# Routing steps spread over the attention passes of a fused attention and expert kernel

## The chip, the cores and the metric

The kernel runs on one core of one Trainium2 chip. The metric is the time of one execution on the device in microseconds (us), the median of several runs. A core has five engines that run at the same time and wait for each other by semaphores: TensorE (PE in the profile, its loads of weights PEld), VectorE (DVE), ScalarE (ACT), GpSimd (POOL) and SyncE (SP), which here only issues transfers. 16 DMA engines move data between the chip's memory (DRAM) and the core's SBUF; transfers are issued by SP, ACT and POOL. Products land in PSUM, from which VectorE and ScalarE read.

## The reference

Two stages. First attention with a mask by blocks, for 8 batches and 8 heads, 576 rows of 64; then a layer of 8 experts over all 4608 tokens (512 wide, the hidden width 1024), in which each token goes to one expert:

```python
scores = scale * np.matmul(q, k.transpose(0, 1, 3, 2))
scores = np.where(block_i >= block_j, scores, -1e9)        # blocks of 64 rows
attn = softmax(scores)                                     # minus the row's maximum, exp, over the sum
x = (attn @ v), heads side by side                         # 8 x 576 x 512
fresh_e = argmax(x[b, s] @ w_gate)
e = fresh_e if s == 0 or sigmoid(x[b, s] @ w_local) < 0.5 else prev_e
p = softmax(x[b, s] @ w_gate)
out[b, s] = p[e] * (relu(x[b, s] @ w1[e]) @ w2[e])
```

The expert of a token can be that of the token before, so the choice is a running recurrence along a batch's tokens.

## The kernel before, in words

**Attention in passes.** A pass works on one batch and a pair of heads: 32 passes (NPR), in a loop over `it` from -2 to 31. In each turn of it three passes are under way: `a = it + 2` is transposed (turns, tails), `c = it + 1` has its row maxima taken (top, mid_maxima, high_maxima), and `e = it` goes through scores, exp (segment, expo) and the products with v (av, L659 and L667); the pass before, `x = it - 1`, is brought back to rows (norm, cast_x, rows_x) and written to a table of rows in DRAM (x_rows). Row maxima are reduced by VectorE out of PSUM (L577 to L581), exchanged between halves of the partitions by GpSimd or VectorE (exchange, L590 to L592), and turned into a diagonal (shift, L599) that TensorE subtracts from the scores. GpSimd also casts the transposed queries to bf16 (halves_in, L992).

**Gate and routing, beside the passes.** Every fourth pass TensorE adds up the gate's sums for the batch (gate_sums, L732). The tokens fall into four groups of 9 x 128 (GC = 9 columns of 128 tokens). For a group the routing is a chain of small operations: gate and fresh (the fresh expert), fresh_b, rows_ps and scan_rows (the recurrence as a scan over rows), carry, chosen (one-hot rows of the chosen expert), ranks, ranks_all and ranks_b (the token's place among its expert's tokens), shares (its weight p), and, for the first two groups together, whole, tile_experts, taken, low1 and high (which slot of which tile a token gets; TensorE inverts the table by products of one-hot rows, inverse, L380).

**The order is written by hand.** The kernel is in manual order: each engine runs its instructions as the program emits them. The dictionary `plan` holds for a pass `it` and a named place a list of pieces, entered with `at(it, place, piece)` and run by `run(it, place)`. In the order of a pass the places are: start, mid (behind the middle maxima, ahead of two segments), top, begin, turned (inside tails), turn, gap (ahead of the last query blocks' products and their norm_last, L541), late (behind norm_last; then come the other products, and in the next pass norm, L533), end, first (TensorE's part of the routing). The pieces of group g begin at pass `i0 = 8 * g + 9 + g // 2`.

**Weights.** The experts' weights come by GpSimd's queue in quarters (weights, load_weights, L63), spread over the passes, the last ones at passes 28 to 30. The last pass also starts the experts: three gathers of rows (gather, L763), DMA transposes (turn_rows, L784), and copies of the first two experts' w1 (first, L779).

**Experts in tiles.** A tile is 128 tokens of one expert. For tile t: gather, turn_rows, first (VectorE copies w1 of an expert whose offset is read at run time), up (32 products, L798), down (8 products with w2 at an offset read at run time, L813), scatter (L822). 36 tiles run in a loop; `steps`, `ahead` and `behind` hold the routing pieces of the later groups for each t; up to 7 more tiles run if they are used.

**Start.** `warm(n)` issues n products of ones into a scratch tile of PSUM (L837) ahead of the first transposes.

Of the kernel before, what the change touches and what calls it, by code (L numbers as in the profile page):

```python
# [16 lines left out]
def kernel(  # L17
# [28 lines left out]
    P = 128  # L46
# [127 lines left out]

    def fresh_b(g):
        best = sm9[:, 1, :]
        nc.vector.tensor_mul(tmp["eq"], tmp["eq"], desc_e[:, None, :].to_broadcast([P, GC, E]))
        nc.vector.reduce_max(best, tmp["eq"], axis=AX)
        nc.vector.tensor_scalar(best, best, -1.0, float(E), op0=ALU.mult, op1=ALU.add)
        nc.vector.tensor_mul(ak[:, 0, :], best, sm9[:, 2, :])  # L180
# [81 lines left out]
    def ranks_all(g):  # L262
        off = sm9[:, 4, 0:E]
        nc.vector.tensor_add(tmp["pf"], tmp["pf"], off[:, :, None].to_broadcast([P, E, GC]))
        nc.vector.tensor_add(tmp["pf"], tmp["pf"], tots[:, 0, :].rearrange("p (e c) -> p e c", c=GC))
        nc.vector.tensor_mul(tmp["pf"], tmp["pf"], ohg(g))

    def ranks_b(g):
        rk = sm9[:, 5, :]
        nc.vector.reduce_sum(rk, over_e(tmp["pf"]), axis=AX)  # L270
        nc.vector.tensor_copy(ints[:, 0, 0, :], rk)
        nc.vector.tensor_single_scalar(ints[:, 1, 0, :], ints[:, 0, 0, :], 7,
# [26 lines left out]

    def per_token(dst, w, n, tmp):  # L300

        nc.vector.tensor_mul(tmp, oh[:, :, 0:n], w[:, :, None].to_broadcast([P, E, n]))
        nc.vector.reduce_sum(dst, over_e(tmp), axis=AX)
# [123 lines left out]
    with tc.manual_schedule():  # L427
# [428 lines left out]
        warm(26)  # L856
# [21 lines left out]
        def low1(g, z):  # L878
            c0, n = GC * g + 5 * z, 5 - z
            low(ohl01[:, c0:c0 + n, :], c0, n)  # L880

        at(29, "first", lambda ps: inverse(ps, None, rhsa, na, NTA))
        for g in range(3):
            i0 = 8 * g + 9 + g // 2
            at(i0, "turn", lambda ps, g=g: gate(g))
            at(i0, "late" if g == 2 else "gap", lambda ps, g=g: fresh(g))
            at(i0 + 1, "gap", lambda ps, g=g: fresh_b(g))
            at(i0 + 1, "first", lambda ps: rows_ps(ps, buf))
            at(i0 + 2, "gap", lambda ps: scan_rows(buf))
# [11 lines left out]
            if g == 2:  # L901
                at(i0 + 5, "gap", lambda ps, g=g: ranks(g))
                at(i0 + 5, "gap", lambda ps, g=g: ranks_all(g))
                at(i0 + 5, "end", lambda ps, g=g: ranks_b(g))
# [5 lines left out]
            at(i0 + 7, "gap", lambda ps, g=g: ranks_b(g))  # L910
            at(i0 + 8 if g else i0 + 7, "late", lambda ps, g=g: shares_b(g))
# [16 lines left out]
        at(30, "turn", lambda ps: weights(2))  # L928
# [8 lines left out]
        for it in range(-2, NPR):  # L937
# [30 lines left out]
            def turns():  # L968

                pw[:] = g_tile(0), g_tile(1)  # L970
                if a == 0:
                    for w in (1, 0):
# [4 lines left out]
                        turned(0, w, pw[w])  # L977
                    return
# [260 lines left out]
        def highb():  # L1239
# [18 lines left out]
                     lambda: fresh_b(last)],  # L1258
# [6 lines left out]
                     lambda: ranks_in(cur[2], dve), lambda: ranks(last), lambda: ranks_all(last)],  # L1265
                 10: [lambda: ranks_b(last), plan2],
# [14 lines left out]
        for t in range(NTM):  # L1281
            for z in (3, 4, 5) if t == 0 else wait_for.get(t, (t + 5,)):
                if z < NTM + 2:
                    gather(z)
            if t + 1 < NTM:
# [8 lines left out]
            for f in ahead.get(t, []) + steps.get(t, []):  # L1294
# [65 lines left out]
```

## Time and profile before

| | |
|---|---|
| median of three runs | 458.43 us (458.36 to 460.65) |
| the profiled execution | 454.2 us, span 452.4 us |
| TensorE busy | 432.8 us (96%) |
| VectorE, ScalarE, GpSimd busy | 315.1, 273.6, 288.5 us |
| mean granted TensorE clock | 0.995 |
| DMA | 71.15 MB, mean 157 GB/s |

The passes run from about 11 us to 304 us of the span, the experts from 305 us to the end. A line of the timeline reads: start and duration in us, engine, line of the kernel, operation, output <- input with sizes, how many are merged, and in brackets how long the engine had been idle and what ended that. In the view by stretches each engine has its busy time and its count of instructions; then come the granted clock (1.00 is full), the share of the DMA engines and GB/s.

### The profile page before, as it was taken

To read this page: it belongs to the slowest core of one execution; us is meant where nothing else is said; L and a number is where in the kernel's file an instruction comes from. 1 tells how busy PE (TensorE), PEld (TensorE's weight loads), DVE (VectorE), ACT (ScalarE), POOL (GpSimd) and SP (SyncE) were. 2 spreads that over 40 slices of the span, in tenths; PEclk is the share of its full clock that TensorE was granted. 3 is DMA by queue.
4 is the path that set the end of the run, shared out by engine and by line. 5 is a ranking of instruction groups with operands and counts; after the bars stand their busy time and mean duration, and the time that the engine had idled before them with its cause. 6 is when DMAs were issued, how large, how long until landed. Compare 5 with 4: busy or idle time off the path is not lost.

```text
span 452.4 us, 19648 instructions
## 1 busy us (share of the span) xinstructions
PE 432.8 (96%) x7738; PEld 338.2 (75%) x7738; DVE 315.1 (70%) x856; ACT 273.6 (60%) x573; POOL 288.5 (64%) x674
## 2 busy tenths in 40 slices
PE   7899999999999999999999999987999999999994
PEld 5688787787788877787878777776676777777772
DVE  4777667768778888887788897954876884333422
ACT  3857766766667657665766666554454555555552
POOL 4556566667566747675556665672777758878853
PEclk8999999999999999999999999999999999999999
DMA  8999699999999975999779898887655665546532
GB/s 152 190 164 188 143 173 164 195 186 171 185 181 175 186 162 117 203 161 183 158 143 184 149 179 152 146 139 104 146 137 153 137 147 149 151 130 167 141 116 80
DMA packets 169885, 71.15 MB, mean 157 GB/s; under 512 B 151424, under 2 KB 158080, under 8 KB 169792
## 3 DMA queue, kind: packets, MB, share of 16 engines
q1 hardware_dynamic: 154640, 38.05, 44.5%
q0 software_dynamic: 13952, 31.52, 34.4%
q8 instruction: 64, 1.05, 1.0%
q10 hardware_dynamic: 1200, 0.30, 0.3%
q14 instruction: 29, 0.24, 0.2%
HBM read 67.18 MB, written 14.97 MB: 182 GB/s over the span
## 4 chain that ended last, share of the span: by engine, by line
PE 41%; DVE 26%; POOL 12%; issue 11%; DMA 5%; ACT 2%; POOLq 1%; DVEq 0%; ACTq 0%
PE g L667 10%; DVE mx L577 9%; PE ps_s L625 8%; POOL out_dram L822 6%; PE ps_s L634 4%; PE ps_h L798 4%; DMA out_dram<-o_sb,tok2s 3%; PE g L659 3%; PE ps_m L558 3%; PE ps_o L813 3%; PE g L951 2%; PE g L732 2%; DVE diag L599 2%; POOL diag L599 1%; DMA x_rows<-w_bf 1%
## 5 line engine op out<-in xcount | busy, mean ns | idle before, releaser
L641 ACT ACTIVATE prob<-ps_s 128x640 f32<-128x640 f32 (+2 forms) x128 | 103.6, 839 | 41.3 <-PE ps_s L634 40.4
L577 DVE TENSOR_REDUCE mx<-ps_m 128x2 f32<-128x640 f32 (+2 forms) x96 | 100.2, 1044 | 26.9 <-PE ps_m L558 19.9
L625 PE MATMUL ps_s<-plb 64*128 64x320 f32 (+4 forms) x768 | 107.3, 400 | 0.7 <-DVE mx L579 0.7
L625 PEld LDWEIGHTS ps_s<-plb 64*128 64x128 f32 x768 | 68.0, 189 | 20.8 <-issue 9.8
L667 PE MATMUL g<-vt,prob 128*64 128x65 f32 x2560 | 80.3, 222 | 0.0
L667 PEld LDWEIGHTS g<-vt,prob 128*64 128x64 f32 x2560 | 77.5, 138 | 0.1
L813 PE MATMUL ps_o<-w_bf,hT 128*128 x304 | 71.5, 380 | 0.0
L802 ACT ACTIVATE hT<-ps_h 128x512 bf16<-128x512 f32 x76 | 45.4, 597 | 26.6 <-PE ps_h L798 26.2
L816 ACT ACTIVATE o_sb<-ps_o,share 128x512 f32<-128x512 f32 x37 | 25.4, 686 | 40.2 <-PE ps_o L813 35.7
L813 PEld LDWEIGHTS <-hT 128*128 128x128 bf16 x304 | 28.0, 98 | 27.8 <-issue 0.3
L590 POOL COPY mx<-mx 64x2 f32<-64x2 f32 x64 | 11.7, 183 | 52.3 <-DVE mx L581 49.7
L779 DVE COPY natb<-w_bf 128x4096 bf16 x20 | 24.7, 1235 | 27.5 <-PE ps_h L798 25.2
L779 DVE COPY plb<-w_bf 128x4096 bf16 x20 | 25.1, 1253 | 24.6 <-PE ps_h L798 24.1
L798 PEld LDWEIGHTS <-plb 128*128 128x128 bf16 x608 | 35.4, 98 | 6.8 <-issue 2.9
L798 PEld LDWEIGHTS <-natb 128*128 128x128 bf16 x608 | 35.4, 98 | 6.2 <-DVE rs L541 1.5
L558 PE MATMUL ps_m<-kh,qh 64*128 64x320 bf16 (+3 forms) x256 | 37.6, 324 | 2.5 <-DVE mx L581 1.4
L634 PE MATMUL ps_s<-diag,ones 64*128 64x448 bf16 (+1 forms) x372 | 36.8, 274 | 2.0 <-DVE diag L599 0.4
L822 POOL DMA_INDIRECT out_dram<-o_sb,tok2s x17 | 28.7, 1690 | 11.6 <-ACT o_sb L816 7.0
L63 POOL DMA_DIRECT2D w_bf<-in_moe_w_dram x56 | 33.4, 596 | 1.4 <-DMA x_rows<-xb 0.4
L987 ACT COPY plb<-g 128x512 f32<-128x512 f32 x62 | 33.2, 593 | 0.3 <-PE g L951 0.2
L651 POOL MEMSET prob<- 64x128 f32 x128 | 24.5, 206 | 11.1 <-ACT prob L641 5.0
L798 PE MATMUL ps_h<-scr,plb 128*128 128x128 bf16 x416 | 25.3, 219 | 2.6 <-DVE share L788 2.3
(285 smaller groups left out, 769.8 us busy)
## 6 DMA issues: line engine op xcount, KB each, us to landing
w_bf<-in_moe_w_dram POOLq DMA_DIRECT2D x48, 256.0 KB, 4.5
vt<-in_v_dram SPq DMA_DIRECT2D x64, 128.0 KB
natb<-in_k_dram SPq DMA_DIRECT2D x63, 128.0 KB
natb<-in_q_dram SPq DMA_DIRECT2D x63, 128.0 KB
w_bf<-in_moe_w_dram POOLq DMA_DIRECT2D x8, 512.0 KB, 5.5
x_rows<-w_bf SPq DMA_DIRECT2D x13, 256.0 KB
natb<-in_k_dram SPq DMA_DIRECT2D x32, 32.0 KB
vt<-in_v_dram SPq DMA_DIRECT2D x32, 32.0 KB
```

Source lines behind the costliest of these rows:

```text
L63: nc.gpsimd.dma_start(out=dst[:, e * WE:(e + 1) * WE].rearrange("p (k f) -> p k f", k=n)[:, r:r + m, :], in_=view[e][:, r:r + m, :])
L558: nc.tensor.matmul(ps[:, h, c:c + w], lhsT=qh[rows(h), 64 * b:64 * b + 128], rhs=kh[rows(h), 0:w], start=True, stop=m is None)
L577: nc.vector.reduce_max(mx[:, b:b + 2], ps[:, :, 0:w], axis=AX)
L625: nc.tensor.matmul(ps[:, h, c:c + n], lhsT=pls[i][rows(h), S + 128 * j:S + 128 * j + 128], rhs=pls[i][rows(h), a:a + n], start=part == 0, ...
L634: nc.tensor.matmul(ps[:, h, c:c + n], lhsT=ones[rows(h), :], rhs=diag[rows(h), a // 64:(a + n) // 64, :], start=False, stop=part == len(SE ...
L641: nc.scalar.activation(p[:, :, SEG0[s]:SEG0[s] + w], ps[:, :, 0:w], func=AF.Exp, scale=scale_attn)
L667: nc.tensor.matmul(g[rows(e), o + 65 * h:o + 65 * h + 65], lhsT=p[:, h, c:c + 64], rhs=t[:, j, h, :], start=(j == 0), stop=(j == m))
L779: nc.vector.tensor_copy(w, w1_bf[:, bass.ds(off, WE)])
L798: nc.tensor.matmul(ps_h[:, f, :], lhsT=w[:, f0 + ko * F:f0 + ko * F + 2 * P - 1:2], rhs=xb[:, ko * P:(ko + 1) * P], start=(ko == 0), stop= ...
L802: nc.scalar.activation(hT[:, half * 4:half * 4 + 4, :], ps_h, func=AF.Relu)
L813: nc.tensor.matmul(ps_o, lhsT=hT[:, fo, :], rhs=w2_bf[:, bass.ds(woff + fo * Dm, Dm)], start=(fo == 0), stop=(fo == FO - 1))
L822: wr = nc.gpsimd.indirect_dma_start(out=out_flat, out_offset=bass.IndirectOffsetOnAxis(ap=g[1][:, g[3]:g[3] + 1], axis=0), in_=o_sb, in_of ...
```

## The change

The pieces of the routing are cut finer and put at other places of the passes, some of them on another engine; a weight load moves, and the start gets more products of ones.

- fresh_b loses its product and its reduce to a new fresh_a. For groups 0 and 1 fresh_a runs in mid, for group 2 in the gap. fresh(2) moves from late to the gap of pass 26, scan_rows(2) from the gap to mid of pass 28.
- ranks_all loses its last product to ranks_own, ranks_b its first two operations to ranks_a. For groups 0 and 1 ranks_own runs in mid, ranks_a in the gap (pass 16 and 25), ranks_b in late of the same pass.
- shares_b of groups 0 and 1 runs on GpSimd.
- low1, the one-hot rows of a token's low part, was one VectorE operation for 5 or 4 columns; it becomes 5 or 4 GpSimd operations of 128 x 128. For group 1 it moves from passes 28 and 29 to late of 26 and 27.
- whole moves from late of 23 to the gap of 24, tile_experts from the gap to mid of 25; taken is cut into four pieces in mid and late of 26 and 27; taken_b moves from late of 27 to the gap of 28.
- The last weight load, weights(2) in the last pass, moves into the expert loop, behind the gather of tile 3 (the fourth).
- At t = 1 of the expert loop the steps run ahead of `sums`.
- At the start half of the first qh is copied by ScalarE instead of VectorE; warm(26) becomes warm(29), and warm(5) and warm(8) stand between and behind the first transposes.

```diff
+    def fresh_a(g):
+        nc.vector.tensor_mul(tmp["eq"], tmp["eq"], desc_e[:, None, :].to_broadcast([P, GC, E]))
+        nc.vector.reduce_max(sm9[:, 1, :], tmp["eq"], axis=AX)
...
+    def ranks_own(g):
         nc.vector.tensor_mul(tmp["pf"], tmp["pf"], ohg(g))
...
-    def shares_b(g):
+    def shares_b(g, eng=nc.vector):
         for j in range(3):
-            nc.vector.tensor_copy(sh[:, :, j], pgs)
+            eng.tensor_copy(sh[:, :, j], pgs)
             if j < 2:
-                nc.vector.tensor_sub(pgs, pgs, sh[:, :, j])
+                eng.tensor_tensor(pgs, pgs, sh[:, :, j], op=ALU.subtract)
...
-            for c in (0, 256):
-                nc.vector.tensor_copy(qh[:, c:c + 256], ps[:, c:c + 256])
+            nc.vector.tensor_copy(qh[:, 0:256], ps[:, 0:256])
+            nc.scalar.copy(qh[:, 256:512], ps[:, 256:512])
...
-        warm(26)
+        warm(29)
...
-            low(ohl01[:, c0:c0 + n, :], c0, n)
+            for c in range(c0, c0 + n):
+                nc.gpsimd.tensor_scalar(ohl01[:, c, :], iota_lo, hl[:, 1, c:c + 1], 0.0,
+                                        op0=ALU.is_equal, op1=ALU.add)
...
-            at(i0, "late" if g == 2 else "gap", lambda ps, g=g: fresh(g))
+            at(i0, "gap", lambda ps, g=g: fresh(g))
+            at(i0 + 1, "gap" if g == 2 else "mid", lambda ps, g=g: fresh_a(g))
...
-            at(i0 + 2, "gap", lambda ps: scan_rows(buf))
+            at(i0 + 2, "mid" if g == 2 else "gap", lambda ps: scan_rows(buf))
...
-            at(i0 + 7, "gap", lambda ps, g=g: ranks_b(g))
-            at(i0 + 8 if g else i0 + 7, "late", lambda ps, g=g: shares_b(g))
+            at(i0 + 7, "mid", lambda ps, g=g: ranks_own(g))
+            at(i0 + 8 if g else i0 + 7, "gap", lambda ps, g=g: ranks_a(g))
+            at(i0 + 8 if g else i0 + 7, "late", lambda ps, g=g: ranks_b(g))
+            at(i0 + 8 if g else i0 + 7, "late", lambda ps, g=g: shares_b(g, nc.gpsimd))
...
-        at(23, "late", lambda ps: whole(False))
+        at(24, "gap", lambda ps: whole(False))
         at(24, "late", lambda ps: whole_b(NTA))
-        at(25, "gap", lambda ps: tile_experts(tea, tend, NTA, tmpta))
-        at(26, "gap", lambda ps: taken(t1ka, hia, na, tmpa))
-        at(27, "late", lambda ps: taken_b(t1ka, hia, na))
-        at(28, "turn", lambda ps: low1(1, 0))
+        at(25, "mid", lambda ps: tile_experts(tea, tend, NTA, tmpta))
+        at(26, "mid", lambda ps: per_token_a(t1, na, tmpa))
+        at(26, "late", lambda ps: per_token_b(t1ka, tmpa))
+        at(26, "late", lambda ps: low1(1, 0))
+        at(27, "mid", lambda ps: per_token_a(dd, na, tmpa))
+        at(27, "late", lambda ps: per_token_b(hia, tmpa))
+        at(27, "late", lambda ps: low1(1, 1))
+        at(28, "gap", lambda ps: taken_b(t1ka, hia, na))
...
-        at(29, "gap", lambda ps: low1(1, 1))
...
-        at(30, "turn", lambda ps: weights(2))
...
                         turned(0, w, pw[w])
+                        warm(5 * w)
...
                 g1 = tails()
+                warm(8)
                 tails_in()
...
             for z in (3, 4, 5) if t == 0 else wait_for.get(t, (t + 5,)):
                 if z < NTM + 2:
                     gather(z)
+                if z == XGB:
+                    weights(2)
...
-            for f in ahead.get(t, []) + steps.get(t, []):
+            for f in steps.get(t, []) + ahead.get(t, []) if t == 1 else ahead.get(t, []) + steps.get(t, []):
                 f()
```

More of the change, by code (lines that the diff above doesn't have):

```diff
@@ L903 @@
                 at(i0 + 5, "gap", lambda ps, g=g: ranks_all(g))
+                at(i0 + 5, "gap", lambda ps, g=g: ranks_own(g))
+                at(i0 + 5, "end", lambda ps, g=g: ranks_a(g))
                 at(i0 + 5, "end", lambda ps, g=g: ranks_b(g))
@@ L1264 @@
                      lambda: new_g(1, lambda ps: ranks_ps(last, ps)),
-                     lambda: ranks_in(cur[2], dve), lambda: ranks(last), lambda: ranks_all(last)],
-                 10: [lambda: ranks_b(last), plan2],
+                     lambda: ranks_in(cur[2], dve), lambda: ranks(last), lambda: ranks_all(last),
+                     lambda: ranks_own(last)],
+                 10: [lambda: ranks_a(last), lambda: ranks_b(last), plan2],
                  11: [plan2_a, lambda: plan2_b(tmp2, hi2)],
```

15 lines of the change are left out of this document (9 added, 6 removed).

## The prediction

> **What bounds the kernel now.** I read the page first (engines, chain), then the timeline pass by pass, then the waits in the two places where the passes end and the experts begin.
>
> ```profile
> PE 432.8 (96%) x7738; PEld 338.2 (75%) x7738; DVE 315.1 (70%) x856; ACT 273.6 (60%) x573; POOL 288.5 (64%) x674
> PE 41%; DVE 26%; POOL 12%; issue 11%; DMA 5%; ACT 2%; POOLq 1%; DVEq 0%; ACTq 0%
> ```
>
> TensorE is busy for 96%, yet the chain that ended last runs over VectorE and GpSimd for 38% of the span: TensorE is the bound with little slack to the other two. So I look for passes that are longer than a clean one. A mark for each pass is the first product of the last query block (L659). Here is a clean pass, 73.43 to 82.02, with VectorE's three waits in it:
>
> ```profile
> 73.43 0.74 PE L659 MATMUL g<-vt,prob 128*64 128x65 f32 x18
> 75.28 0.18 DVE L541 RECIPROCAL rs<-g 128x3 f32<-128x3 f32 x1 [1.11 <-PE g L667]
> 76.61 0.20 DVE L533 RECIPROCAL rs<-g 128x6 f32<-128x6 f32 x1 [0.56 <-PE g L667]
> 79.13 1.23 DVE L577 TENSOR_REDUCE mx<-ps_m 128x2 f32<-128x1024 f32 x1 [0.54 <-PE ps_m L558]
> 82.02 0.80 PE L659 MATMUL g<-vt,prob 128*64 128x65 f32 x20
> ```
>
> 8.59 us. VectorE idles 1.11 us in the place that the plan calls "gap", 0.56 us in "late", 0.54 us in "mid". Routing work in gap and late is free up to 1.67 us together; beyond that it pushes L533 (3.18 us after the mark here). The mid wait is a product's latency and stays when VectorE is late, so work of 0.5 us there is free, while a late L533 lengthens the pass one for one. The marks where routing runs (the pass after each mark):
>
> ```profile
> 109.02 0.80 PE L659 MATMUL g<-vt,prob 128*64 128x65 f32 x20
> 118.38 0.80 PE L659 MATMUL g<-vt,prob 128*64 128x65 f32 x20
> 227.66 0.56 PE L659 MATMUL g<-vt,prob 128*64 128x65 f32 x11
> 237.25 0.80 PE L659 MATMUL g<-vt,prob 128*64 128x65 f32 x20
> 247.34 0.80 PE L659 MATMUL g<-vt,prob 128*64 128x65 f32 x20
> 256.77 0.80 PE L659 MATMUL g<-vt,prob 128*64 128x65 f32 x20
> 265.87 0.80 PE L659 MATMUL g<-vt,prob 128*64 128x65 f32 x20
> 274.81 0.81 PE L659 MATMUL g<-vt,prob 128*64 128x65 f32 x20
> 285.39 0.80 PE L659 MATMUL g<-vt,prob 128*64 128x65 f32 x20
> 294.63 0.80 PE L659 MATMUL g<-vt,prob 128*64 128x65 f32 x20
> 93.75 1.22 PE g L732 x30
> ```
>
> The last row is the gate sums, 1.22 us of TensorE in every fourth pass (it = 24 and 28 here). Above 8.59, or 9.81 with sums: it 10 +0.77, it 23 +1.00, 24 +0.28, 25 +0.84, 26 +0.51, 27 +0.35, 28 +0.77, 29 +0.65. The check of the reading is the pass from 247.34: the next fence has its L533 at 251.42, 4.08 after the mark, 0.90 later than in the clean pass, and the pass is 0.84 longer.
>
> **The change, part by part.**
>
> *Routing pieces off VectorE's gap and late.*
>
> ```profile
> 109.86 1.24 DVE L177 TENSOR_TENSOR scr<-scr,desc_e 128x72 f32<-128x72 f32 x1
> 231.26 0.23 DVE L266 TENSOR_TENSOR scr<-scr,oh 128x72 f32<-128x72 f32 x1
> 251.42 0.19 DVE L533 RECIPROCAL rs<-g 128x6 f32<-128x6 f32 x1
> 275.46 0.82 DVE L366 TENSOR_TENSOR ohl<-hl,iota_lo 128x640 bf16<-128x640 f32 x1
> 277.24 0.41 DVE L193 TENSOR_TENSOR_SCAN scr<-scr,zeros 9x128 f32<-9x128 f32 x1
> ```
>
> - it 10: fresh_a (the 1.24 us product and a reduce) leaves the gap for mid; the two small operations and this step's transposes on TensorE stay. Of +0.77 I take away 0.45.
> - it 15 and 23: the product of ranks_own leaves late (0.23 and its spacing, 0.26 each); from it 23 also whole's three smaller operations (under L266's 0.23 each; 0.46 together). 0.26 + 0.72.
> - it 24: ranks leaves the gap, whole's half microsecond comes in, whole_b stays in late under the sums: the 0.28 goes, less 0.03: 0.25.
> - it 25: the table's three operations go from the gap to mid, behind a stretch with sums, where there is room; ranks_a's two come into the gap; shares_b's five small dependent operations go to GpSimd, ranks_b's three come into late (two fewer, about 0.4). With the gap's relief L533 comes back nearly to 3.18: 0.80 of 0.84.
> - it 28 and 29: the one-hot rows (0.82 in it 28, the smaller one in it 29) leave VectorE. In it 28 taken_b's five small operations come into the gap, which they fit. 0.72 of 0.77; in it 29 0.31 of 0.65, since the inverse's products and the carry stay.
>
> - it 26 and 27: the four operations of taken go in pairs to mid and late (a reduce of 144 elements in late is covered by its 0.56); fresh and fresh_a stand in the gap, as much as it holds. it 27 keeps its +0.35, which its transposes on TensorE would set anyway. 0 beyond what follows.
>
> Sum: 0.45 + 0.26 + 0.72 + 0.25 + 0.80 + 0.72 + 0.31 = 3.5 us less. A piece costed at nothing in mid (ranks_own twice, per_token_a twice) is covered by the 0.54; without that cover each costs its length (0.23 for L266, the others wider).
>
> What mid costs: scan_rows in it 28 is two scans of 0.41 and a memset (about 0.9 us, over the 0.5 by 0.4), and an operation with two inputs there holds up GpSimd's exchange that starts at the same time (fence below). I take +0.6 for both, between 0 and 1.5 (every mid piece in full beyond the 0.54).
>
> *One-hot rows on GpSimd.* Eighteen operations of 128x128 (5 in it 17, 4 in 18, 5 in 26, 4 in 27) stand behind the pass's second weight load and ahead of the exchange of the next pass's middle maxima, whose chain (exchange, L599, the cast of qh) TensorE waits for without slack.
>
> ```profile
> 78.73 0.18 POOL L590 COPY mx<-mx 64x2 f32<-64x2 f32 x1 [1.40 <-DVE mx L581]
> 82.45 0.29 POOL L1036 CAST qh<-plb 128x128 bf16<-128x128 f32 x1
> 176.56 0.79 POOL L591 COPY mx<-mx 64x2 f32<-64x2 f32 x1
> 179.34 0.18 POOL L590 COPY mx<-mx 64x2 f32<-64x2 f32 x1 [0.20 <-DVE mx L581]
> ```
>
> No row shows such an operation on GpSimd. Lower end: 0.18 (L590's); nearest in shape: 0.29 (the 128-column cast); upper: 0.79 (L591, a copy that usually takes 0.18 and stood behind VectorE's 0.82 us one-hot). I take 0.27 start to start, just under the cast, since independent ones overlap: 1.35 us for five. In a clean pass GpSimd has 1.40 us free ahead of the exchange (78.73). In it 17 the gate stands there too, and 0.20 us are left (179.34); 0.61 come back, since L591 is no longer held, and about 0.36 go, since VectorE delivers earlier: room 0.45, so the five make the exchange 0.9 late. VectorE's own lateness in this pass goes (0.82 in late against 0.56 of idle time, about 0.3): net +0.6. In it 26, which has the gate as well, +0.51 becomes +0.9: +0.4. In it 18 and 27 there is no gate, and four fit into 1.40: 0. Together +1.0 (at 0.18 an operation about +0.1, at 0.5 +4.5).
> [...]
>
> *The last weight rows behind the fourth gather.*
>
> ```profile
> 299.00 0.79 POOL L63 DMA_DIRECT2D w_bf<-in_moe_w_dram  x1
> 302.04 1.86 POOL L763 DMA_INDIRECT xg<-x_rows,toka  x1 [0.16 <-issue]
> 305.08 1.11 PE L798 MATMUL ps_h<-scr,natb 128*128 128x128 bf16 x17 [1.42 <-DMA scr<-scr]
> 309.30 0.89 PE L798 MATMUL ps_h<-scr,plb 128*128 128x128 bf16 x13 [2.27 <-DVE share L788]
> 311.89 1.90 PE L813 MATMUL ps_o<-w_bf,hT 128*128 x8
> L813 PEldq EVENT_SEMAPHORE  x2: 51/51/51, 310.5 to 310.7; - x2
> DMA to landing us min/median/max: 4.1/4.5/5.5
> ```
>
> TensorE waits 1.42 us for the first transposed rows and 2.27 us before the second tile (VectorE's share is not read by it, so I take this to be the second transpose too). The 512 KB load of 299.0 is in the queues just then. Without it both tiles could follow at once: 3.7 us. But the first L813 reads a slice at an offset known only at run time, so it waits for every load of w2 (the two semaphore events stand ahead of the first L813 alone), and everything on TensorE stands behind it. The load now starts behind the gather of 302.04, at about 304.2, and lands 5.5 us later, 309.7, or up to 311.5 beside the other transfers; gathers 4 and 5 are pushed by about 0.8 and are wanted later. (304.2 is 302.04 + 1.86 and 0.3 for the issue.) So L813 moves from 311.89 to 309.8 at best. I take 310.5: -1.4, between -2.1 and +1.0.
>
> *Table work ahead of the sums (t = 1), and ones in the gaps of the start.*
>
> ```profile
> 316.30 0.52 DVE L744 TENSOR_TENSOR lgS<-g,lgS 128x128 f32<-128x128 f32 x2 [3.79 <-PE g L732]
> 320.25 1.23 DVE L779 COPY natb<-w_bf 128x4096 bf16 x1 [0.26 <-issue]
> 322.06 1.95 PE L798 MATMUL ps_h<-scr,natb 128*128 128x128 bf16 x32 [0.46 <-DVE tmp L302]
> 3.90:7.31 3.41, 2.07 (x21) 1.26 (x21) 0.76 (x2) 1.85 (x7) 0.10 (x1) 1.00 1.30 193
> 7.31:10.73 3.42, 3.42 (x30) 1.86 (x26) 2.50 (x5) 0.36 (x1) 2.30 (x9) 0.50 0.72 154
> 10.71 1.23 DVE L577 TENSOR_REDUCE mx<-ps_m 128x2 f32<-128x1024 f32 x1 [0.74 <-PE ps_m L558]
> ```
>
> whole_b and the shares go into VectorE's 3.79 us of idling; the copy of 320.25 starts over 2 us earlier and TensorE's 0.46 us goes: -0.4 (0 to -0.5).
> At the start the granted clock is 0.50 from 7.31 to 10.73 (the last columns are clock, DMA, GB/s), after 3.41 us in which TensorE was busy for 2.07. Sixteen more products of ones (3, 5 and 8; 0.056 each, as seventeen of that shape take 1.11 at 305.08) bring some 0.9 us into that stretch. With the clock full VectorE's 0.74 us wait goes; the eight ahead of the first scores cost up to 0.45. Half of qh runs on ScalarE beside VectorE's half; no row prices that, and I leave it inside the range. I take -0.5, between -1.2 and +0.4.
> [...]
>
> **Sum:** -3.5 + 0.6 + 1.0 - 1.4 - 0.4 - 0.5 = -4.2 us. The profiled execution took 454.2 us (span 452.4 and 1.8 around it), 4.2 less than the median of the runs, 458.43. The terms are differences inside one execution, and behind the passes TensorE runs without a gap, so I subtract them from the median: 454.2 us, -0.9%.
>
> **Rivals.**
> 1. The seam gives nothing, since L813 waits for the moved load (landing at 311.5 to 312) or the second transpose lands as late as before. For it: the two semaphore events; against: 5.5 us of landing. Seam 0 to +0.8: 455.6 to 456.4.
> 2. GpSimd becomes the bound (slower than before): each one-hot operation takes 0.79 as L591 did. The five run 3.5 us past their room of 0.45, the four 1.8 past 1.4: 10.6 us instead of my 2 x 0.9, so 458.4 - 4.2 + 8.8 = 463. It decides against the change from 0.54 us an operation: 2 x (5 x 0.54 - 0.45) + 2 x (4 x 0.54 - 1.4) - 0.83 = 5.2, all the rest of the sum. [...]
> 3. The pieces don't move out of the way: mid is no idle stretch, because the chain runs through it. Each mid piece then costs its length: fresh_a 0.5 twice, ranks_own 0.25 twice, per_token_a (two larger products) about 0.33 twice, scan_rows 0.9, together 3.1 instead of 0.6: 456.7. Against it: 0.54 us in a clean pass, after TensorE's product.
>
> **How the numbers follow.** Forecast 0.51 (own range 452.3 to 455.6), rival 1 0.21, rival 2 0.14, rival 3 0.14. This kernel's runs spread by 0.5% (458.36 to 460.65), 2.3 us; that is my bound for no change, 456.1 to 460.7. Faster: 0.51, most of rival 1 (0.12) and little of rival 3 (0.02), 0.65. Slower: rival 2 with over 0.67 us an operation and the tails, 0.12. Same: the rest, 0.23. The best ends of all terms (mid 0, one-hot rows +0.1, seam -2.1, sums -0.5, start -1.2) give -7.2, 451.2; I set that as low, and 459.0 high, which leaves out rival 2's upper part and the tails, under 2 in 10.
>
> **What would show it.** Right: the passes after marks 10, 15, 23, 25 and 28 within 0.35 of 8.59 (9.81); those of it 17 and 26 longest, with GpSimd's one-hot rows directly ahead of L590; both expert waits under 0.5 us and a new one ahead of the first L813; no stretch at 0.50 behind 7.3; no wait at the fifth tile. Wrong: one-hot rows above 0.5 us, VectorE's L577 without its wait behind a mid piece and the pass longer, or L813 not earlier against the gather.

## The result, and the profile after

| | before | after |
|---|---|---|
| median of the runs | 458.39 us | 465.01 us |
| ratio | | 1.0117, 95% 1.0074 to 1.0159 |
| the profiled execution | 454.2 us, span 452.4 | 462.77 us, span 461.1 |
| VectorE, GpSimd busy | 315.1, 288.5 us | 308.7, 295.2 us |

The change makes the kernel slower by 1.2%; a second measurement of the same pair (below) gave 1.0086, 1.0061 to 1.0111. One of the four runs after lay in a slower state of the chip and the ratio leaves it out: the other three have a median of 463.85 us. The forecast was 454.2 us, 0.9% faster. On the page of the changed kernel (busy time of each engine, then the chain that ended last):

```profile
PE 436.3 (95%) x7754; PEld 340.8 (74%) x7754; DVE 308.7 (67%) x841; ACT 271.4 (59%) x574; POOL 295.2 (64%) x702
PE 51%; DVE 15%; POOL 12%; issue 11%; DMA 6%; ACT 3%; POOLq 1%; DVEq 0%; ACTq 0%
```

VectorE did lose its place in the chain (26% before, 15% now) and 6.4 us of work; still the span grew. The timeline of the changed kernel says where. L670 is the line of the pass marks (L659 before):

```profile
109.56 0.63 PE L670 MATMUL g<-vt,prob 128*64 128x65 f32 x14
118.47 0.80 PE L670 MATMUL g<-vt,prob 128*64 128x65 f32 x20
174.07 0.80 PE L670 MATMUL g<-vt,prob 128*64 128x65 f32 x20
185.56 0.63 PE L670 MATMUL g<-vt,prob 128*64 128x65 f32 x14
194.94 0.80 PE L670 MATMUL g<-vt,prob 128*64 128x65 f32 x20
231.10 0.80 PE L670 MATMUL g<-vt,prob 128*64 128x65 f32 x20
239.95 0.28 PE L670 MATMUL g<-vt,prob 128*64 128x65 f32 x2
249.84 0.34 PE L670 MATMUL g<-vt,prob 128*64 128x65 f32 x4
258.52 0.80 PE L670 MATMUL g<-vt,prob 128*64 128x65 f32 x20
270.67 1.35 PE L670 MATMUL g<-vt,prob 128*64 128x65 f32 x20
280.18 0.80 PE L670 MATMUL g<-vt,prob 128*64 128x65 f32 x20
306.89 0.75 PE L670 MATMUL g<-vt,prob 128*64 128x65 f32 x20
```

Passes 10, 23 and 25 came down as forecast (8.91, 8.85 and 8.68 us against a clean 8.59). Pass 17 takes 11.49, 18 takes 9.38, 26 takes 12.15 and 27 takes 9.51: 8.17 us over four clean passes, 1.50 before. The last mark is 5.6 us later than before (306.89 against 301.28). Pass 17 in the timeline, with GpSimd's rows and the TensorE row that waits for them (L892 is the one-hot row, L601 the exchange, L625 VectorE's first operation behind the exchange, L1013 the cast of qh; rows may overlap where several are merged):

```profile
178.96 1.44 POOL L892 TENSOR_SCALAR ohl<-iota_lo,hl 128x128 bf16<-128x128 bf16 x2
179.68 2.78 POOL L892 TENSOR_SCALAR ohl<-iota_lo,hl 128x128 bf16<-128x128 bf16 x4
182.53 0.18 POOL L601 COPY mx<-mx 64x2 f32<-64x2 f32 x1
182.99 0.16 DVE L625 TENSOR_TENSOR mx<-mx 128x1 f32<-128x1 f32 x1 [1.44 <-POOL mx L602]
184.12 0.60 POOL L1013 CAST qh<-plb 128x512 bf16<-128x512 f32 x1
184.77 0.31 PE L569 MATMUL ps_m<-kh,qh 64*128 64x320 bf16 x2 [3.00 <-POOL qh L1013]
```

Five operations fill GpSimd from 178.96 to 182.47, 0.70 us each; the exchange follows at once, then shift and cast, and TensorE stands still for 3.00 us. The view of waits (us in total, times, longest) names the same chain, and one new wait for the weight load:

```profile
PE ps_m L569 <- POOL qh L1013: 6.6, 3, 3.0
PE ps_o L824 <- DMA w_bf<-in_moe_w_dram: 2.5, 1, 2.5
```

The start of the experts in the changed kernel (L63 the moved load, L809 first layer, L824 second layer):

```profile
309.12 0.78 POOL L63 DMA_DIRECT2D w_bf<-in_moe_w_dram  x1
309.55 0.62 PE L809 MATMUL ps_h<-scr,natb 128*128 128x128 bf16 x8
311.35 0.83 PE L809 MATMUL ps_h<-scr,plb 128*128 128x128 bf16 x12
314.16 1.04 PE L824 MATMUL ps_o<-w_bf,hT 128*128 x4
317.65 1.02 PE L824 MATMUL ps_o<-w_bf,hT 128*128 x4 [2.45 <-DMA w_bf<-in_moe_w_dram]
318.72 1.50 PE L809 MATMUL ps_h<-xb,natb 128*128 128x128 bf16 x24
323.01 1.17 PE L809 MATMUL ps_h<-scr,plb 128*128 128x128 bf16 x18
326.53 1.67 PE L809 MATMUL ps_h<-scr,natb 128*128 128x128 bf16 x27
```

Both first-layer waits are gone, the second layer's first four products run, and the fifth waits for the load, which lands 8.5 us after its issue. The third tile starts 11.83 us behind the last mark, 12.34 before; the fifth 3.52 us behind the fourth, 4.14 before. After that the profiled execution loses about 4 us for which the profile shows no cause (from the fourth tile's last product to the last product of all it takes 124.8 us); a second trace of the same kernel takes 120.9 there, as before the change, so the change does not bring them every time.

### The profile page after: what moved, and what is told of

Same layout as the page of the kernel before. It is cut to its first block, busy times and chain, and to the rows that moved or that the text cites. A ratio compares the mean times of both kernels' runs of the same rounds, so it can differ in the third digit from the quotient of the medians.

```text
span 461.1 us, 19695 instructions
## 1 busy us (share of the span) xinstructions
PE 436.3 (95%) x7754; PEld 340.8 (74%) x7754; DVE 308.7 (67%) x841; ACT 271.4 (59%) x574; POOL 295.2 (64%) x702
## 4 chain that ended last, share of the span: by engine, by line
PE 51%; DVE 15%; POOL 12%; issue 11%; DMA 6%; ACT 3%; POOLq 1%; DVEq 0%; ACTq 0%
PE g L678 12%; PE ps_s L636 8%; DVE mx L588 7%; PE ps_h L809 6%; PE ps_o L824 5%; PE ps_s L645 4%; PE g L670 4%; PE ps_m L569 3%; DMA out_dram<-o_sb,tok2s 3%; POOL out_dram L833 3%; PE g L971 2%; PE g L743 2%; POOL ohl L892 2%; POOL scr L774 2%; POOL xg L774 2%
## 5 line engine op out<-in xcount | busy, mean ns | idle before, releaser
L678 PE MATMUL g<-vt,prob 128*64 128x65 f32 x2560 | 81.4, 222 | 0.5 <-issue 0.4
L824 PE MATMUL ps_o<-w_bf,hT 128*128 x304 | 71.8, 379 | 2.8 <-DMA w_bf<-in_moe_w_dram 2.5
L813 ACT ACTIVATE hT<-ps_h 128x512 bf16<-128x512 f32 x76 | 43.9, 596 | 40.2 <-PE ps_h L809 23.2
L824 PEld LDWEIGHTS <-hT 128*128 128x128 bf16 x304 | 28.0, 98 | 31.4 <-issue 4.1
L809 PEld LDWEIGHTS <-natb 128*128 128x128 bf16 x608 | 35.5, 98 | 6.6 <-issue 2.5
L809 PEld LDWEIGHTS <-plb 128*128 128x128 bf16 x608 | 35.5, 98 | 5.1 <-issue 1.1
L601 POOL COPY mx<-mx 64x2 f32<-64x2 f32 x64 | 11.8, 185 | 42.4 <-DVE mx L592 36.8
L63 POOL DMA_DIRECT2D w_bf<-in_moe_w_dram x56 | 33.4, 597 | 1.5 <-DMA x_rows<-xb 0.4
L833 POOL DMA_INDIRECT out_dram<-o_sb,tok2s x17 | 19.8, 1165 | 19.8 <-ACT o_sb L827 14.8
L662 POOL MEMSET prob<- 64x128 f32 x128 | 23.5, 200 | 13.6 <-ACT prob L652 8.2
L610 POOL TENSOR_TENSOR diag<-negi,mx 128x384 bf16<-128x384 f32 x31 | 25.7, 828 | 2.6
```

What stands on the lines that cost most here:

```text
L63: nc.gpsimd.dma_start(out=dst[:, e * WE:(e + 1) * WE].rearrange("p (k f) -> p k f", k=n)[:, r:r + m, :], in_=view[e][:, r:r + m, :])
L678: nc.tensor.matmul(g[rows(e), o + 65 * h:o + 65 * h + 65], lhsT=p[:, h, c:c + 64], rhs=t[:, j, h, :], start=(j == 0), stop=(j == m))
L809: nc.tensor.matmul(ps_h[:, f, :], lhsT=w[:, f0 + ko * F:f0 + ko * F + 2 * P - 1:2], rhs=xb[:, ko * P:(ko + 1) * P], start=(ko == 0), stop= ...
L813: nc.scalar.activation(hT[:, half * 4:half * 4 + 4, :], ps_h, func=AF.Relu)
L824: nc.tensor.matmul(ps_o, lhsT=hT[:, fo, :], rhs=w2_bf[:, bass.ds(woff + fo * Dm, Dm)], start=(fo == 0), stop=(fo == FO - 1))
L833: wr = nc.gpsimd.indirect_dma_start(out=out_flat, out_offset=bass.IndirectOffsetOnAxis(ap=g[1][:, g[3]:g[3] + 1], axis=0), in_=o_sb, in_of ...
```

## The experiments

All ratios are to the kernel before on the same chip (its medians were 455.3 to 455.9 there). The passes of the traces, in us over the clean 8.59 (9.81 with sums), by the same marks:

| kernel | 1 to 9 | 17, 18 | 26, 27 | 28, 29 | last mark to the end of the second tile |
|---|---|---|---|---|---|
| before | 0.29 | 0.64 | 0.86 | 1.42 | 16.81 |
| after; again | 1.08; 2.38 | 3.69; 4.80 | 4.48; 4.80 | 0.85; 0.60 | 16.29; 15.54 |
| load_back; again | 3.75; 2.58 | 4.79; 4.77 | 4.77; 4.79 | 0.60; 0.59 | 16.87; 13.51 |
| low_only | 3.08 | 4.53 | 4.94 | 0.44 | 19.77 |
| low_dve | 3.84 | 0.64 | 1.23 | 0.65 | 19.48 |
| both_back | 1.63 | 0.64 | 1.24 | 0.66 | 18.76 |
| load_only; again | 1.92; 2.73 | 0.64; 0.64 | 0.85; 0.88 | 1.44; 1.45 | 19.36; 19.90 |
| load_only_fill | 0.64 | 0.63 | 0.85 | 1.42 | 17.27 |
| no_start | 2.28 | 0.66 | 1.24 | 0.45 | 15.36 |
| split_load | 2.87 | 0.78 | 1.23 | 0.66 | 14.03 |
| spread | 1.76 | 0.33 | 0.34 | 0.83 | 15.87 |
| spread_old_start | 2.49 | 0.32 | 0.33 | 0.77 | 16.29 |
| all_three | 1.30 | 0.32 | 0.36 | 0.83 | 13.80 |

The first and the last column vary between executions (load_back's last column is 16.87 and 13.51, and over the kernels with the load in the last pass it goes from 13.51 to 19.77), so a single trace does not price the place of the load.

**One-hot rows and load, each undone, both undone, rows alone.** low_dve:

```diff
         def low1(g, z):
...
-            for c in range(c0, c0 + n):
-                nc.gpsimd.tensor_scalar(ohl01[:, c, :], iota_lo, hl[:, 1, c:c + 1], 0.0,
-                                        op0=ALU.is_equal, op1=ALU.add)
+            low(ohl01[:, c0:c0 + n, :], c0, n)
```

> The changed kernel with the one-hot rows (low1) back in one VectorE operation, at the changed kernel's places (late of passes 17, 18, 26, 27). Theory 1 (the one-hot rows on GpSimd are the loss: about 0.70 us each, so five or four of them make the exchange and the cast of qh late): the passes after marks 17, 18, 26, 27, which were 2.90, 0.79, 3.56 and 0.92 us over a clean pass, come back to about 0.3, 0.3, 0.9 and 0.6 (VectorE's 0.82 us now stands in late beside a reduce), 6 us less than the changed kernel: 459. Theory 2 (the loss sits at the moved weight load and in what the experts do behind it; 3.8 us of TensorE's unexplained waits stand there in the changed kernel's trace): the four passes get shorter but the time falls by less than 2 us against the changed kernel or the expert tiles keep all of the 3.8 us.

load_back, and both_back with both edits:

```diff
+        at(30, "turn", lambda ps: weights(2))
...
-                if z == XGB:
-                    weights(2)
```

> The changed kernel with the last weight load back in the last attention pass. Theory 1 (one-hot rows): same time as the changed kernel within 1 us; the waits ahead of the first two tiles come back (1.4 and 2.3 us) and the wait of 2.45 us inside the first tile's second products goes, together 0 to +0.7. Theory 2 (moved load): 3 to 5 us less than the changed kernel, and TensorE's unexplained waits behind tile 13 gone.

> Both undone: one-hot rows on VectorE and the load in the last pass; what is left are the routing pieces off VectorE's gap and late, the table work ahead of the sums and the start. Theory 1: 6 us less than the changed kernel and 1.5 to 3 us less than the kernel before (455.5 to 457), by the passes after marks 10, 15, 23, 25, 29 as they stand in the changed kernel's trace (3.3 us less than before), the sums (0.6 less), and a VectorE one-hot operation that costs about 0.6 in pass 26. Theory 3 (cutting the routing pieces costs elsewhere what it gains, in the waits for the rows' writes that the changed kernel's trace shows in four passes): the same as the kernel before.

low_only is the kernel before with the GpSimd loop in low1, at late of 17, 18, 26 and 27:

> The kernel before with only the one-hot rows on GpSimd, in late of passes 17, 18, 26 and 27. Theory 1: the four passes take about 2.9, 0.8, 3.5 and 0.9 us over a clean one (0.3, 0.3, 0.5, 0.35 in the kernel before), passes 28 and 29 lose 0.7 and 0.3, and the time is 5 to 6 us over the kernel before (464). Theory 2: 1 us over or less.

Measured: low_dve 0.9984 (0.9947 to 1.0022), load_back 1.0145 (1.0052 to 1.0238), both_back 0.9928 (0.9891 to 0.9965), low_only 1.0132 (1.0052 to 1.0212). Marks 17, 18, 26 and 27 of low_dve:

```profile
178.98 0.80 PE L670 MATMUL g<-vt,prob 128*64 128x65 f32 x20
187.89 0.28 PE L670 MATMUL g<-vt,prob 128*64 128x65 f32 x2
...
260.34 0.80 PE L670 MATMUL g<-vt,prob 128*64 128x65 f32 x20
269.55 0.63 PE L670 MATMUL g<-vt,prob 128*64 128x65 f32 x14
```

8.91 and 9.21 us where the changed kernel took 11.49 and 12.15: theory 1 holds for the rows, and low_only shows that they alone cost 1.3% (0.5 to 2.1). load_back gained nothing, so theory 2 falls. Without both parts the rest is a gain of 0.7%, so theory 3 falls. But low_dve lies 0.6% above both_back (their intervals just overlap): with the rows on VectorE the load seems to cost too, while load_back shows no cost of its place beside the rows on GpSimd. That was not expected and led to the later runs.

**The price by itself.** On both_back, pairs of one form in late of the passes 1 to 8, where GpSimd has room; extra work, written over later:

```diff
+        at(1, "late", price(lambda o: gp.tensor_scalar(o, iota_lo, nth, 0.0, op0=ALU.is_equal, op1=ALU.add)))
+        at(2, "late", price(lambda o: gp.tensor_scalar(o, iota_lo, 3.0, 0.0, op0=ALU.is_equal, op1=ALU.add)))
+        at(3, "late", price(lambda o: gp.tensor_scalar(o, iota_lo, nth, None, op0=ALU.mult)))
...
```

> The price of GpSimd's operation by itself, two of a kind in late of the passes 1 to 8 (extra work, its results are written over later): compare with a scalar for each partition and an addition; compare with a constant; one multiplication by a scalar for each partition; a product of two inputs; a plain copy; the first with f32 input; the first on 32 columns; compare alone. Theory A (GpSimd computes a 128x128 bf16 operation with arithmetic in 0.70 us whatever VectorE does): all tensor-scalar forms 0.65 to 0.75, the copy 0.3, 32 columns about 0.3. [...] Theory C (the second operation or the scalar's kind makes it): compare alone or with a constant at 0.3 to 0.4.

The groups by line, engine and form (busy us, then mean ns of one; L900 to L907 are the eight forms in the order of the text above), and below them the gate's row of the kernel before:

```profile
L900 POOL TENSOR_SCALAR ohl<-iota_lo,nth 128x128 bf16<-128x128 bf16 x2 | 1.5, 744 | 0.1
L905 POOL TENSOR_SCALAR ohl<-id_f,nth 128x128 bf16<-128x128 f32 x2 | 1.4, 718 | 0.1
L901 POOL TENSOR_SCALAR ohl<-iota_lo 128x128 bf16<-128x128 bf16 x2 | 1.3, 643 | 0.1
L902 POOL TENSOR_SCALAR ohl<-iota_lo,nth 128x128 bf16<-128x128 bf16 x2 | 1.2, 612 | 0.1
L907 POOL TENSOR_SCALAR ohl<-iota_lo,nth 128x128 bf16<-128x128 bf16 x2 | 1.2, 602 | 0.1
L906 POOL TENSOR_SCALAR ohl<-iota_lo,nth 128x32 bf16<-128x32 bf16 x2 | 0.8, 396 | 0.1
L903 POOL TENSOR_TENSOR ohl<-iota_lo,nth 128x128 bf16<-128x128 bf16 x2 | 0.8, 390 | 0.1
L904 POOL COPY ohl<-iota_lo 128x128 bf16<-128x128 bf16 x2 | 0.5, 289 | 0.0
```

```profile
L159 POOL TENSOR_SCALAR ak<-lg 128x9 f32<-128x9 f32 x4 | 1.2, 290 | 0.3
```

Theory A mostly holds: the change's form (L900) takes 0.74 us, with f32 input 0.72, the comparison alone 0.60, a multiplication alone 0.61, on 32 columns 0.40; the two widths give about 0.28 fixed and 3.6 ns a column (an estimate from 744 ns at 128 columns and 396 at 32). A copy of the same tile takes 0.29, a product of two inputs 0.39. Theory C explains 0.14 of it at most. VectorE's work beside it is not what makes it long: in the changed kernel the eighteen take 0.70 to 0.76 us, 0.715 on average, and the last of the five in pass 17 takes 0.71 although VectorE is idle beside it (its L625 at 182.99 ends 1.44 us of idling). L159 is an instruction of this kind (a comparison with a constant and an addition) that stood in the trace of before: 0.29 us for 9 columns.

**The rows where there is room.** On both_back:

```diff
...
+        for z in range(3):
+            at(19 + z, "late", lambda ps, z=z: low1(3 * z, 3))
...
+        at(27, "late", lambda ps: low1(9, 2))
+        at(27, "late", lambda ps: low1_gp(11, 2))
+        at(28, "late", lambda ps: low1_gp(13, 2))
+        at(29, "mid", lambda ps: low1(15, 3))
...
```

> One-hot rows in small pieces: VectorE takes three columns in late of 19, 20 and 21, two in late of 27 and three in mid of 29; GpSimd takes two in late of 27 and two in late of 28, where its room of 1.40 us holds two operations of 0.70; the load in the last pass. Theory 1 (room by place): the passes after marks 17 and 18 fall from 0.32 over to 0, 26 from 0.62 to 0.3, 27 from 0.61 to 0.45, 28 and 29 unchanged; 1.0 us less than the kernel with both undone: 0.9% under the kernel before. Theory 2 (GpSimd's room is less than two operations, or mid is none): 27, 28 or 29 grow by 0.5 to 1.4 and nothing is gained, 0.4 to 0.7% under.

Measured 0.9949 (0.9915 to 0.9983). By its marks the passes do as theory 1 says but for 18, which stays at 0.32 (0.01 in 17, 0.00 and 0.34 in 26 and 27, 28 and 29 together 0.17 more): 1.0 us less than both_back over these six. Two GpSimd operations of 0.70 nearly fit where the room is 1.40: pass 28 is 0.17 us longer. The time does not tell it from both_back, and by itself it is theory 2's (0.5% under; 0.9% lies outside the interval); 1 us is below what these runs resolve.

**The start.** no_start is both_back with the start as before:

```diff
-            nc.vector.tensor_copy(qh[:, 0:256], ps[:, 0:256])
-            nc.scalar.copy(qh[:, 256:512], ps[:, 256:512])
+            for c in (0, 256):
+                nc.vector.tensor_copy(qh[:, c:c + 256], ps[:, c:c + 256])
...
-        warm(29)
+        warm(26)
...
-                        warm(5 * w)
...
-                warm(8)
```

> The kernel with one-hot rows on VectorE and the load in the last pass, and the start as it was before (products of ones and the cast of qh). Theory 1 (the start is worth the forecast 0.5): 0.5 us more than with the new start, 0.6% under the kernel before. Theory 2 (the first passes wait for their transfers, whatever the start does): the same as with the new start, 0.7% under the kernel before.

0.9941 (0.9909 to 0.9973) against 0.9928: no difference that these runs resolve (the forecast 0.5 us is 0.1%). Its clock was full from 7.31 to 10.73 without the added products:

```profile
7.31:10.73 3.42, 3.14 (x26) 1.97 (x28) 2.60 (x5) 0.73 (x3) 1.61 (x8) 1.00 0.64 142
```

The half clock of before's trace at that place was that execution's, and the added products do not prevent one: in the first 20 us a stretch at half clock stands in three of nine traces with the new start (low_dve from 14.31, load_back, prices) and in two of eight with the old one. The first pass mark stands at 20.7 us on average with the new start and at 20.6 with the old one, so the traces show no gain either.

**The load alone, and the wait filled.** load_only is the kernel before with the load behind the fourth gather:

> The kernel before with only the last weight load moved behind the fourth gather. Theory 1 (the place of the load is worth what the changed kernel's trace shows, the end of the first tile's second products 11.78 us after the last pass mark instead of 12.51): 0.5 to 1 us less than the kernel before. Theory 2 (the load's landing sets the start of the experts; 8 us from issue to landing, 2.45 and 3.27 us of TensorE's waiting in the two traces that have it): 1 to 3 us more than the kernel before, as the distance between the two kernels with VectorE's one-hot rows (2.7 us) says.

Measured 1.0063 (1.0032 to 1.0093): theory 2. First its timeline, then the view by stretches of 3.41 us (busy time and count of PE, PEld, DVE, ACT, POOL; then granted clock, DMA share, GB/s):

```profile
304.73 0.79 POOL L63 DMA_DIRECT2D w_bf<-in_moe_w_dram  x1
308.88 1.04 PE L813 MATMUL ps_o<-w_bf,hT 128*128 x4
313.81 1.86 PE L813 MATMUL ps_o<-w_bf,hT 128*128 x4 [3.89 <-DMA w_bf<-in_moe_w_dram]
```

```profile
308.65:312.06 3.41, 1.27 (x9) 0.57 (x9) 2.66 (x7) 0.82 (x3) 0.00 (x0) 0.99 0.94 88
312.06:315.47 3.41, 1.66 (x5) 0.55 (x5) 0.00 (x0) 0.00 (x0) 0.00 (x0) 0.50 0.64 159
315.47:318.88 3.41, 3.41 (x33) 3.35 (x31) 0.00 (x0) 1.28 (x2) 1.89 (x2) 0.51 0.38 109
```

The load lands 9.1 us after its issue and TensorE waits 3.89 us. From 312.06, still inside the wait, the clock is at half for 6.8 us: the next tile takes 5.9 us. The changed kernel's trace has a wait of 2.45 and a full clock there. So the same kernel was run with the wait filled by products of ones:

```diff
             for fo in range(FO):
+                if t == 0 and fo == FO // 2:
+                    for _ in range(55):
+                        nc.tensor.matmul(ffn["ps_o"][1][:, 0:P], lhsT=ones, rhs=ones,
+                                         start=True, stop=True)
```

> The kernel before with the moved load once more, as the partner of the next run: 0.6% over the kernel before, TensorE's wait inside the first tile's second products 2.4 to 4 us and, where it is over 2 us in one stretch of 3.41 us, one or two stretches of 3.41 us at a granted clock of 0.50 behind it.

> The same with 55 products of ones (about 3.1 us) between the fourth and the fifth product of the first tile's second layer, into a bank that the next tile writes over; they run while TensorE waits for the load, and nothing else is changed. Theory 1 (a long wait of TensorE costs a second time, by the stretches at half clock behind it): no stretch at 0.50 behind the wait, the tile behind it back from 5.9 to about 4.3 us, and 1 to 2.5 us less than without the products (0 to 0.3% over the kernel before). Theory 2 (only the wait itself costs, and the half clock is incidental): the same as without the products or 0.5 us more.

Without the products 1.0050 (1.0019 to 1.0081), with a wait of 4.06 us in the trace and 6.8 us at half clock from 315.27; with them 1.0015 (0.9982 to 1.0048). The trace with them (L815 the products of ones, L817 the second layer):

```profile
303.53 0.79 POOL L63 DMA_DIRECT2D w_bf<-in_moe_w_dram  x1
309.83 1.95 PE L815 MATMUL ps_o<-ones 128*128 128x128 bf16 x32
312.91 1.02 PE L817 MATMUL ps_o<-w_bf,hT 128*128 x3 [1.13 <-DMA w_bf<-in_moe_w_dram]
```

```profile
307.68:311.09 3.41, 3.36 (x52) 2.94 (x51) 2.36 (x7) 0.58 (x2) 0.00 (x0) 1.00 0.96 83
311.09:314.50 3.41, 2.23 (x30) 1.69 (x28) 0.00 (x0) 0.53 (x1) 0.00 (x0) 1.00 0.77 172
```

The load lands as late (9.4 us), the clock stays full, the next tile takes 4.3 us, and 1.6 us of time come back by the ratios (0.0035 of 456). The intervals overlap, so the time alone would not prove it. But the granted clock is on record for every run: the twelve with the products have 0.996 on average, the twelve without 0.990. With the traces that shows theory 1: the long wait cost a second time here, through the clock.

**The load in halves; the parts once more; the best of them.** split_load is both_back with one half in the last pass and one behind the fourth gather:

```diff
-        at(30, "turn", lambda ps: weights(2))
+        at(30, "turn", lambda ps: weights(1))
...
+                if z == XGB:
+                    weights(1)
```

> Both parts undone, but the last load cut in two: one half (256 KB) in the last pass, the other behind the fourth gather. Theory 1 (what costs is the late landing, 8 to 9 us from issue for 512 KB): the half lands about 5 to 6 us after its issue, TensorE's wait inside the first tile's second products falls from 2.5 to 3.9 us to 1 us or less and comes later in it, and the time is within 0.3% of the kernel with both undone. Theory 2 (any load behind the fourth gather stands behind the transposes and lands as late): the wait of 2 to 4 us stays and the time is 0.5% over the kernel with both undone (0.2% under the kernel before or more).

0.9911 (0.9873 to 0.9949), and better than theory 1: in its trace no product of the second layer waits for a load, and the first tile waits 1.06 us for its rows. By `load_weights` the half behind the gather holds only the rows that the last two of the eight products can read (L824; the trace holds seven of its eight).

```profile
303.26 0.61 POOL L63 DMA_DIRECT2D w_bf<-in_moe_w_dram  x1
304.38 1.95 PE L809 MATMUL ps_h<-scr,natb 128*128 128x128 bf16 x32 [1.06 <-DMA scr<-scr]
308.75 1.90 PE L824 MATMUL ps_o<-w_bf,hT 128*128 x7
```

> The changed kernel once more, beside the same kernel with the load back, so that the two parts can be added up on one chip. Additive theory: 0.7% under the kernel before without both parts, one-hot rows +1.4 to +2.0%, load +0.6%: 1.3 to 1.9% over the kernel before. Rival (the parts hide each other): 1.0% over or less. If the 3.8 us of unexplained waits of TensorE behind tile 13 belong to the change, they are in this trace too; if not, tiles go at 3.51 us there.

> The changed kernel with the load back in the last pass. Additive theory: 0.6% less than the changed kernel beside it. Rival: the same as the changed kernel or slower (the first measurement of it, four runs, said 0.3% slower).

after_again 1.0086 (1.0061 to 1.0111), load_back_again 1.0135 (1.0070 to 1.0201): the parts do not add up (0.7% less, 2.1% more for the rows by load_back, 0.6% more for the load would be 2.0% over). Beside the late rows the moved load cost nothing that either measurement shows; both traces of that kernel show the shorter wait (2.5 us) at full clock. The 4 us without a cause are not in after_again's trace.

spread_old_start is spread with the start as before; all_three has the load in halves as well:

> One-hot rows in pieces, load in the last pass, start as before: what the parts say is the best of them. Additive theory: 1.0 us less than the kernel with the old start and rows in four places: 0.75% under the kernel before. Rival (parts this small are lost in the first passes' waits for transfers, which vary by 3 us between runs): 0.5 to 0.7% under, not to be told from the others.

> One-hot rows in pieces, the start as before, and the load in two halves: 1 us for the pieces, 1 to 1.8 us for the halves. Additive theory: 1.0 to 1.3% under the kernel before. Rival: 0.7 to 0.9%, as the single ones.

0.9891 (0.9830 to 0.9952), which tells neither theory from the other, and 0.9861 (0.9814 to 0.9908), which fits the additive one. all_three, with the pieces off VectorE, the one-hot rows in small portions and the load in halves, beats both kernels: 449.47 us beside 455.63 before.

## Why the prediction was wrong, by its steps

- **Pieces off gap and late: right in the passes named.** Forecast -3.5 and +0.6 for what mid costs, -2.9 together. Passes 10, 15, 23, 24, 25, 28 and 29 changed by -0.45, -0.41, -0.74, -0.20, -0.75, -0.21 and -0.36, together -3.1, the scans in mid of 28 included; in low_dve, without GpSimd's rows, 28 came to -0.40. Pass 15 is the weak one: with the same pieces it is 0.00 to 1.44 us over clean in other traces. Over all the passes 10 to 29 the gain is less: 7.5 us over clean on average in the four traces with the old pieces, 5.7 in the five with the new ones and the rows on VectorE in four places, 1.8 us, since pass 11 waits more in some traces (0.28 to 1.77 over clean) and 26 and 27 are 0.4 longer with the rows there. Rival 3 (mid is no idle stretch) falls: pass 25 holds the table work in mid and is 0.09 over clean.
- **One-hot rows on GpSimd: the step that failed.** I wrote that no row showed such an operation, and took 0.27 us from a cast of the same shape; each takes 0.70 to 0.76. Gate's L159 is an operation of this kind, 0.29 us at 9 columns, so 0.29 was a floor at a fourteenth of the width, not the value. The chain behind it held (the five overran GpSimd's room, the exchange and the cast came late, TensorE waited): with 0.70, rival 2's formula gives 2 x (3.5 - 0.45) + 2 x (2.8 - 1.4) - 0.83 = 8.1 us more, and the four passes grew by 6.7 in the first trace and by 8.1 in the second (9.60 against 1.50). That the second agrees so well is partly luck: the formula has no term for the clock, and passes 17 and 18 are 3.69 us over clean where no half clock follows the wait (first trace) and 4.80 where it does (second). Rival 2 happened, by the operation's own length (0.71 us also with VectorE idle beside it) and not behind an operation of VectorE's as L591's 0.79, and I had given it 0.14.
- **Casts and tensor-scalar operations on GpSimd.** The cast was no measure for the one-hot row. Casts took 0.29 us for 128 columns in the kernel before and 0.60 for 512, by these two 0.8 ns a column (an estimate); a tensor-scalar operation took 0.60 to 0.74 for 128 columns (3.6 ns a column by the estimate from the run prices), where VectorE made 640 columns of one-hot rows in 0.82. In some rows operations of VectorE and GpSimd took longer side by side: GpSimd's L591 0.79 and 0.68 us instead of 0.18 beside VectorE's L366 in the kernel before (176.56 and 185.47), and VectorE's L610 0.85 instead of about 0.2 in the changed kernel where the late exchange pushed GpSimd's L610 on top of it (183.39 and 267.83). No run shows what does this, and the price of the eighteen does not need it. Of the hold-up that the forecast had in mid little came: the changed kernel's longest GpSimd row of an exchange takes 0.32 us, L601 beside the scan of pass 28 (276.87), the others up to 0.23.
- **Seam: -1.4 forecast, by itself +2.3 to +2.9 us (0.50 and 0.63%).** Both waits ahead of the first layers went, as I had said, in the changed kernel. Three things were wrong. The landing: 5.5 us was the median of the 512 KB loads in the passes; behind the fourth gather it took 7.6 to 9.4 in six traces, and even in the last pass 6.8 to 8.3 in the four traces that show it. The product that waits: not the first, since the first four run and the fifth waits; the moved load holds only rows that the last four can read. And what the wait itself costs, since I had no term for the clock behind it. In the changed kernel's trace the change still gave 0.5 us there.
- **Sums: right, -0.6** for -0.4 (0 to -0.5); the fifth tile no longer waits, in any trace with the new order.
- **Start: -0.5 forecast, nothing found.** The half clock that I meant to remove stood at that place in one execution only, and later ones in the first 20 us came with either start. no_start and low_only, both with the old start, had a full clock from 7.31 to 10.73, with TensorE busy for 2.69 and 2.31 us in the 3.41 us ahead of it, against 2.07 in before's trace.

The forecast's -4.2 and the measured +5.4 us (the ratio 1.0117) differ by 9.6 us, and by 8.1 with the second measurement (+3.9). Against the forecast +1.0 the rows account for 5.7 in the first trace and 7.1 in the second, the clock behind their waits included. The rest, seam and start, I can't split exactly. Why the load costs in one company and not in the other stays open: the moved load is followed by 6.8 us at half clock in low_dve and both traces of load_only and by none in both traces of the changed kernel, but half clock stands at the seam of both_back, load_back and low_only too, where the load is in the last pass.

## What to carry to other kernels

Price an operation by a row of the same instruction, even at another width, before one of another instruction at the same width; two widths give the fixed part and the slope. A row at one small width is only a floor (0.29 us at 9 columns here, 0.70 to 0.76 at 128); a few of the operations as extra work, in a place with room, give the price. Before work goes to an engine that is idle on average, write down its room in that very place, in us, and divide by the price: here it was two operations, not five. A late transfer behind gathers landed 2 to 4 us later here than the median of its kind (7.6 to 9.4 us against 5.5); cut in halves on either side of the gather it cost nothing that these runs resolve.

## What the runs showed of the hardware

In these traces a wait of TensorE was paid again where it left little work in one stretch of 3.41 us. Half clock came in such stretches, in the kernel before from 7.31 to 10.73, in the changed kernel from 268.60 to 272.01, in load_only two in a row (312.06 to 318.88). In the first two executions it came back at 451.05 and 459.75, 130 and 56 times 3.413 us after those starts, so I count on in these steps through the full clock between. In load_back around the wait of pass 17 (same columns as above):

```profile
185.35:188.76 3.41, 0.84 (x18) 0.53 (x18) 1.56 (x4) 1.05 (x6) 3.01 (x10) 1.00 1.39 205
188.76:192.17 3.41, 3.41 (x66) 3.41 (x66) 1.75 (x6) 1.77 (x2) 2.93 (x10) 0.50 0.76 111
```

Pass 18 is 1.88 over clean there and 0.79 in the changed kernel, where the wait of 3.00 us fell across two stretches (1.91 and 1.92 us busy by counting on from the one at half clock) and neither is followed by half clock. Laid on the grid of each trace's own half-clock stretches, the 17 traces say more (up to 439 us, by the records that they hold). All 15 stretches at full clock with up to 1.4 us of TensorE work were followed by half clock; of the 23 with 1.4 to 2.1 us six were, the 2.07 at the start of the kernel before among them, so busy time alone is no threshold there; none with more was. Of these 15 stretches only one was idle throughout (both_back, 303.75 to 307.17).

The early passes (1 to 9) varied from 0.29 to 3.84 us over clean between traces, by waits for input transfers and for the rows' writes; before's profiled execution happened to have the least.
